# A state-space scan with a two-layer block: prefix products in one scan, W_out parts by adding transfers, a new order on every engine

## The chip, the core and the metric

The kernel runs on one core of a Trainium2 chip. The core has TensorE (PE; its weight loads are listed apart as PEld), VectorE (DVE), ScalarE (ACT), GpSimd (POOL) and SyncE (SP), which here only issues transfers. Each engine takes its instructions in the order of its own queue and waits at semaphores for the others. The metric is the device time of one execution in microseconds (us); the median of three runs of the kernel before is 332.77 us (331.59 to 333.74).

## What is computed

```python
# x (4, 8, 768, 32), a (4, 8, 768), B and C (4, 8, 768, 16)
log_a = np.log(np.clip(a, 1e-06, 1.0))
for c in range(nc):                                   # chunks of 32 steps
    cum = np.cumsum(la, axis=-1)
    L = np.exp(cum[:, :, :, None] - cum[:, :, None, :]) * causal
    CB = np.einsum('bhin,bhjn->bhij', Cc, Bc)
    y_intra = np.einsum('bhij,bhjd->bhid', CB * L, xc)
    y_inter = np.einsum('bhin,bhnd->bhid', Cc, state) * np.exp(cum)[:, :, :, None]
    y[:, :, sl] = y_intra + y_inter
    Bx = np.einsum('bhjn,bhjd->bhjnd', Bc, xc) * np.exp(cum[:, :, -1:] - cum)[:, :, :, None, None]
    state = np.exp(np.sum(la, axis=-1))[:, :, None, None] * state + np.sum(Bx, axis=2)
# then, on (4 * 768, 8 * 32) = (3072, 256)
h = x @ w_in                                          # (256, 2048)
g = h * (1.0 / (1.0 + np.exp(-h)))
out = g @ w_out                                       # (2048, 256)
```

## The kernel before

The sequence of 4 x 768 steps is cut into 12 *units* of 256 steps (four chunks of 64), three units to a batch row. The state goes from unit to unit within a row. Two units make a *pair* of 512 columns for the two layers; pair 0 is units 0 and 1.

**The order.** The whole program is written out as one list of tokens, SCHEDULE. A token such as "E,3,0" calls one small function, which issues a few instructions on one engine; each engine's queue is the list's order, cut down to its own instructions. A second table, SLOTS, says which buffer of a pool each tile takes ("s2k": 49 of 2 KB a partition, "r4k": 12, "raw": 7, "hp": 3 in PSUM).

**A unit.** "La" loads the decays (from the scratch tensor "az" in DRAM), "Ln", "Lt" and "Lx" load B, C and x, on SP's queue for the most part. "E" makes the decay masks by a scan on DVE (line 511), "T" transposes B or C on DVE (524), "B" (519) and "C" (550) scale B and C by decays on POOL, "ce" copies C for even and odd heads on ACT (545, with the constant "par"). On PE, "g0" makes the scores (584), "D" and "gd" the state's additions (570), "Y" the outputs (634 and 643). On DVE, "M" multiplies masks and scores (599) and "S" steps the state (614). For units 0 and 1 the decays are not loaded from "az" but made on the chip from a small load of "a": "A", "AT", "AU", "as", "ab" (445, 450, 454, 494 and 496, 501).

**Prefix products.** "P" (481 to 487) makes a unit's prefix products of the decays, with a 1 ahead of every chunk, by one scan on DVE over 128 partitions and 260 columns: "Lp" loads the clipped decays into "pz" (one buffer) from the scratch tensor "ac", and the scan writes "pfx" (one buffer). "ac" is filled by four "AD" stores on POOL's queue from "acp", which "AA" clips on POOL. There are ten such scans, for units 2 to 11. Units 0 and 1 have their own ("P01").

**Weights.** w_in and w_out come as 64-bit floats, in eight pieces of 512 KB each ("lw,0" to "lw,15", the first eight of them w_in). A piece goes through "u" and "v" on ACT (294, 297), "w,n,0", "w,n,1" and "w,n,2" on DVE (303, 307, 310) and "W" on POOL (318) to become 32-bit floats. For products at full pace each piece is then split in three parts: high "H" on ACT (322), low "lD" and third "dD" on DVE (326, 330).

**Layers.** Pair 0's first layer runs in plain 32 bits: "s" (696), 12 groups of 8 products, and its second layer "n1" (760), 64 products, all but two pieces of w_in, which go as for the later pairs. From there each pair has eight steps "a" (8 products, 799, high and low parts), "ax" on ACT (810), "d" (4 products, third part), "dg" (silu, 820) and "h" (826) on ACT, "l" (650) and "e" (836) on DVE, and then "q" (781): three products for each of 2 x 8 x 2 groups, in the accumulators "hp" and "o_ps". "Va" and "Vd" add the accumulators up, "o" (714) transposes, "O" stores. The last half pair is turned over on PE ("Vt", "ot", "or", "os", lines 726 to 749).

**Fillers.** "z" issues products of a tile of zeros into "o_ps": its first number is how many wide ones (128 x 512, line 438), the second how many narrow ones (64 x 64, line 440).

**Names on the path of the prediction.** The first weight step, the first scan of unit 0, its second mask product ("M,0,0"), the first group of first-layer products ("s,0,0"), unit 1's scan ("E,1,0"), and the fourth group of first-layer products, with which an unbroken run of first-layer products begins.

Of the kernel before, what the change touches and what calls it, by code (L numbers as in the profile page):

```python
# [35 lines left out]
T,3,0 Ln,3,0,1,0 Lx,3,1,0 Lp,3,0 P,3 n1,2,1 Ln,3,0,0,0 B,3 gd,3 w,12,2 W,12 Lt,4,0,0,0 lD,6 y,2,1 xh,2 g0,3 M,3,0 b,3,1
C,3 b,3,0 n1,10,1 n1,3,0 a,0,6 w,10,1 W,10 Lt,4,0,3,0 lD,0 S,3,0 S,3,1 M,3,1 dD,6 n1,11,0 H,13 S,3,2 Lp,4,0 w,14,0
Lt,4,1,0,0 w,14,1 Lx,4,1,0 ax,0,6 n1,10,0 x,2,1 H,15 SM,3,0 d,0,6 w,14,2 H,8 n1,5,0 La,4,1,0 n1,9,0 x,2,0 lD,5 La,4,0,0
E,4,0 Ln,4,0,1,0 dg,0,6 SM,3,1 Y,3 y,3,1 y,3,0 xh,3 lD,3 W,14 H,14 n1,13,0 n1,12,0 T,4,1 ce,4,0 n1,5,1 lD,9 n1,9,1 x,3,0
a,1,0 ax,1,0 n1,13,1 dD,5 Lt,4,0,2,0 x,3,1 n1,8,1 Lt,4,0,1,0 T,4,0 lD,1 ce,4,1 S,3,3 dD,0 d,1,0 P,4 C,4 n1,11,1 E,4,1  # L40
dg,1,0 lD,8 n1,12,1 dD,8 H,10 Lt,5,0,1,0 g0,4 Lx,4,0,0 Ln,4,0,0,0 B,4 H,4 gd,4 b,4,0 dD,1 M,4,1 b,4,1 S,4,0 S,4,1 S,4,2
SM,4,1 n1,4,0 M,4,0 Lt,5,1,1,0 SM,4,0 lD,4 Lt,5,1,0,0 lD,2 S,4,3 dD,2 h,1,0 dD,3 l,1,0 e,1,0 n1,8,0 n1,4,1 Vn,0 lD,10
Y,4 y,4,0 n1,0,1 y,4,1 a,1,1 xh,4 dD,10 H,12 lD,12 Vn,1 Lt,5,0,0,0 ax,1,1 a,1,2 ax,1,2 Lt,5,1,2,0 d,1,1 dg,1,1
Ln,5,0,0,0 Lt,5,1,3,0 T,5,1 La,5,1,0 o,0,0,2 q,1,0,0,1 La,6,1,0 ce,5,1 La,5,0,0 Ln,5,0,1,0 d,1,2 dg,1,2 h,1,2 ce,5,0
Lt,6,1,2,0 a,1,3 ax,1,3 q,1,0,1,1 a,1,4 ax,1,4 d,1,3 dg,1,3 Lp,5,0 q,1,0,1,0 E,5,1 E,5,0 B,5 o,0,1,2 lD,13 AD,2 lD,11
dD,4 Lx,5,0,0 l,1,2 e,1,2 d,1,4 dg,1,4 q,1,2,1,0 q,1,0,0,0 Lt,5,0,2,0 Lt,5,0,3,0 T,5,0 lD,15 dD,12 g0,5 x,4,1 Lx,5,1,0
Ln,6,0,0,0 gd,5 P,5 M,5,1 h,1,4 h,1,1 l,1,4 q,1,2,0,1 a,1,5 q,1,2,1,1 e,1,4 q,1,4,0,1 q,1,2,0,0 La,6,0,0 b,5,0 S,5,0
AD,3 Lt,6,1,1,0 q,1,4,0,0 b,5,1 ax,1,5 d,1,5 Ln,6,0,1,0 S,5,1 S,5,2 SM,5,0 M,5,0 SM,5,1 dD,13 Lt,6,1,3,0 x,4,0 q,1,4,1,1
q,1,4,1,0 C,5 dD,9 dg,1,5 h,1,5 Y,5 Lp,6,0 y,5,1 l,1,1 y,5,0 e,1,1 q,1,1,1,1 a,1,7 O,0,0,2,1,0 l,1,5 Lt,6,1,0,0
q,1,1,0,1 q,1,1,0,0 ax,1,7 e,1,5 d,1,7 Lt,6,0,0,0 xh,5 q,1,5,1,0 E,6,1 Lx,6,0,0 q,1,5,0,1 dg,1,7 Lt,6,0,3,0 T,6,1 ce,6,1  # L50
P,6 x,5,0 ce,6,0 Lt,6,0,2,0 Lt,6,0,1,0 T,6,0 q,1,5,0,0 E,6,0 h,1,7 C,6 g0,6 B,6 M,6,1 Lx,6,1,0 gd,6 b,6,0 Lt,7,1,2,0
h,1,3 q,1,1,1,0 S,6,0 M,6,0 dD,15 b,6,1 q,1,5,1,1 a,2,1 ax,2,1 S,6,1 S,6,2 SM,6,1 a,1,6 ax,1,6 l,1,7 e,1,7 q,1,7,0,0
q,1,7,0,1 d,1,6 dD,11 x,5,1 Lt,7,0,1,0 q,1,7,1,1 q,1,7,1,0 dg,1,6 d,2,1 l,1,3 e,1,3 lD,14 q,1,3,0,0 h,1,6 Lt,7,1,3,0
q,1,3,0,1 SM,6,0 l,1,6 dg,2,1 h,2,1 Y,6 La,7,1,0 y,6,0 e,1,6 Lt,7,1,0,0 Lx,7,1,0 S,6,3 Lt,7,1,1,0 T,7,1 ce,7,0 y,6,1
xh,6 Lt,8,1,0,0 q,1,3,1,1 dD,14 a,2,0 ax,2,0 q,1,6,1,0 q,1,6,1,1 ce,7,1 q,1,6,0,0 l,2,1 d,2,0 Ln,7,0,0,0 dg,2,0 h,2,0
Lp,7,0 P,7 O,0,1,2,0,0 e,2,1 q,1,6,0,1 x,6,1 Va,1,1 x,6,0 q,1,3,1,0 Lt,7,0,2,0 Vd,1,1 o,1,1,2 Lx,7,0,0 a,2,3 ax,2,3
Va,1,0 Vd,1,0 a,2,2 Lt,7,0,3,0 q,2,1,0,1 q,2,1,0,0 l,2,0 o,1,0,2 e,2,0 ax,2,2 d,2,2 q,2,1,1,0 d,2,3 q,2,0,0,0 dg,2,3
q,2,0,1,1 dg,2,2 h,2,2 q,2,1,1,1 La,7,0,0 E,7,0 Lt,7,0,0,0 O,0,1,2,2,0 O,0,0,2,3,0 q,2,0,0,1 C,7 T,7,0 g0,7 Ln,7,0,1,0
E,7,1 B,7 h,2,3 gd,7 b,7,0 M,7,1 O,0,1,2,3,0 q,2,0,1,0 a,2,5 b,7,1 ax,2,5 S,7,0 S,7,1 M,7,0 l,2,2 e,2,2 La,8,0,0 a,2,4
# [67 lines left out]
def kernel(  # L127
# [231 lines left out]
    def pz01(u):  # L359
        return held(f"pz{u}", [128, 4, Q + 1])  # L360
# [527 lines left out]
```

## Time and profile before

| | |
|---|---|
| median of three runs | 332.77 us (331.59 to 333.74) |
| the profiled execution's own time | 333.58 us |
| its span, from the first instruction to the last | 331.8 us |
| TensorE clock granted, mean over the span | 0.985 |
| PE instructions, DVE, ACT, POOL | 3078, 350, 309, 64 |
| read from DRAM, written to it | 22.81 MB, 3.34 MB |
| DVE, longest waits in total | 28.9 us for ACT at line 650, 8.0 us for PE at line 599 |
| last transfers to the output, from issue to landing | 1.8 us |

The profile shows one execution. A group's row gives its busy time and the mean length of one instruction, then the idle time of its engine just ahead of it and what ended that. Products are pipelined: one of 512 columns is listed with some 390 ns, and the next may start long before it ends. So the pace of products is read from the length of a run of them in the chain that ended last, and not from the mean.

### The profile page before, as it was taken

Reading aid. Unit: us, or ns where it says so; the run is one execution under the profiler, and the core shown is the slowest. Engines: PE = TensorE matmul, PEld = TensorE weight load, DVE = VectorE, ACT = ScalarE, POOL = GpSimd, SP = SyncE. Lnnn points to the kernel's source line nnn. Section 1 sums busy time; section 2 is a strip of 40 time slices with the busy share of each in tenths; the row PEclk is TensorE's granted clock in tenths of the full one; section 3 lists DMA queues with packets and bytes.
Section 4 is the critical chain, followed back from the end, with each engine's and each line's share of the span. In section 5 each row is a group of like instructions: output and inputs, shape, how many; then the busy total and the mean of one; then the engine's idle time right before and its main releaser. Section 6 shows DMA issues by size and latency. Waiting matters only on the chain.

```text
span 331.8 us, 7522 instructions
## 1 busy us (share of the span) xinstructions
PE 321.9 (97%) x3078; PEld 244.0 (74%) x3078; DVE 250.8 (76%) x350; ACT 204.9 (62%) x309; POOL 48.6 (15%) x64
## 2 busy tenths in 40 slices
PE   6799999999999999999999999999999999999995
PEld 2478874455587878787887887877888787878884
DVE  4887899999999989698966678956486845453663
ACT  4669787644777565766566677726576367674811
POOL 2435565341111010010010100010000000000000
PEclk9769999999999999999999999999999999999999
DMA  5999478342253311245227241250003300031002
GB/s 173 218 276 256 173 202 197 63 94 34 69 117 69 73 48 21 53 109 123 29 38 152 73 89 30 38 111 2 2 9 70 58 2 0 2 54 18 2 0 63
DMA packets 93522, 26.64 MB, mean 80 GB/s; under 512 B 79840, under 2 KB 86752, under 8 KB 93488
## 3 DMA queue, kind: packets, MB, share of 16 engines
q1 hardware_dynamic: 90960, 25.71, 34.3%
q10 hardware_dynamic: 2352, 0.26, 0.6%
q8 instruction: 24, 0.39, 0.5%
q0 software_dynamic: 176, 0.20, 0.3%
q14 instruction: 10, 0.08, 0.1%
HBM read 22.81 MB, written 3.34 MB: 79 GB/s over the span
## 4 chain that ended last, share of the span: by engine, by line
PE 78%; DVE 12%; DMA 4%; ACT 2%; issue 1%; SPq 1%; POOL 1%; DVEq 0%; POOLq 0%
PE hp L781 27%; PE ga L799 15%; PE gb L799 15%; PE o_ps L781 5%; PE hp L696 5%; PE hp L760 3%; DVE ab L511 3%; PE ga L634 2%; PE ga L584 2%; PE ga L643 1%; DVE ab L599 1%; DMA bn<-in_B_dram 1%; DVE s2k L330 1%; DVE s2k L326 1%; DMA tbc<-in_C_dram 1%
## 5 line engine op out<-in xcount | busy, mean ns | idle before, releaser
L781 PE MATMUL hp<-r4k,s2k 128*128 128x512 f32 x400 | 109.5, 394 | 0.0
L781 PEld LDWEIGHTS hp<-r4k,s2k 128*128 128x128 f32 x400 | 74.0, 188 | 16.4 <-issue 0.5
L650 DVE SCALAR_TENSOR_TENSOR r4k<-r4k,r4k 128x1024 fp32r<-128x1024 f32 (+1 forms) x42 | 50.4, 1199 | 36.6 <-ACT r4k L826 28.9
L799 PE MATMUL ga<-raw,s2k 128*128 128x512 f32 x240 | 62.1, 394 | 0.0
L799 PE MATMUL gb<-raw,s2k 128*128 128x512 f32 x240 | 62.0, 393 | 0.1
L799 PEld LDWEIGHTS gb<-raw,s2k 128*128 128x128 f32 x240 | 44.5, 188 | 11.6 <-ACT gb L810 1.2
L799 PEld LDWEIGHTS ga<-raw,s2k 128*128 128x128 f32 x240 | 44.6, 188 | 11.3 <-ACT ga L810 1.2
L836 DVE SCALAR_TENSOR_TENSOR r4k<-r4k,r4k 128x1024 fp32r<-128x1024 f32 x40 | 48.7, 1222 | 4.9 <-PE o_ps L781 1.5
L826 ACT ACTIVATE r4k<-r4k 128x1024 fp32r<-128x1024 f32 x40 | 41.9, 1057 | 2.0 <-PE hp L781 0.5
L810 ACT ACTIVATE ga<-ga 128x1024 f32<-128x1024 f32 x21 | 21.2, 1009 | 20.5 <-PE ga L799 20.5
L820 ACT ACTIVATE r4k<-gb 128x1024 f32<-128x1024 f32 x21 | 21.5, 1025 | 15.6 <-PE gb L799 15.4
L810 ACT ACTIVATE gb<-gb 128x1024 f32<-128x1024 f32 x21 | 21.2, 1008 | 15.6 <-PE gb L799 15.6
L820 ACT ACTIVATE r4k<-ga 128x1024 f32<-128x1024 f32 x21 | 21.5, 1024 | 15.0 <-PE ga L799 13.8
L781 PE MATMUL o_ps<-r4k,s2k 128*128 128x512 f32 x80 | 30.7, 390 | 0.0
L760 PE MATMUL hp<-r4k,s2k 128*128 128x512 f32 x64 | 30.1, 602 | 0.0
L318 POOL TENSOR_TENSOR s2k<-s2k,s2k 128x512 uint32<-128x512 uint32 (+1 forms) x19 | 24.1, 1280 | 22.6 <-DVE s2k L310 13.7
L519 POOL TENSOR_TENSOR BT<-bn,ab 128x256 f32<-128x256 f32 x10 | 7.3, 730 | 120.3 <-DVE ab L511 87.5
L511 DVE TENSOR_TENSOR_SCAN ab<-ab,diag 128x512 f32<-128x512 f32 x20 | 24.8, 1246 | 0.0
L696 PE MATMUL hp<-r4k,s2k 128*128 128x256 f32 x96 | 22.9, 395 | 0.0
L696 PEld LDWEIGHTS hp<-r4k,s2k 128*128 128x128 f32 x96 | 18.7, 199 | 3.4 <-issue 0.4
L760 PEld LDWEIGHTS hp<-r4k,s2k 128*128 128x128 f32 x64 | 11.6, 189 | 10.8 <-issue 9.3
L599 DVE TENSOR_TENSOR ab<-gb,ab 128x512 f32<-128x512 f32 x12 | 8.2, 686 | 12.3 <-PE gb L584 7.4
(123 smaller groups left out, 390.9 us busy)
## 6 DMA issues: line engine op xcount, KB each, us to landing
ab<-az SPq DMA_DIRECT2D x20, 256.0 KB, 4.2
raw<-in_moe_w_in_dram SPq DMA_DIRECT2D x8, 512.0 KB, 4.1
raw<-in_moe_w_out_dram SPq DMA_DIRECT2D x8, 512.0 KB
out_dram<-r4k SPq DMA_DIRECT2D x44, 64.0 KB, 2.9
xt<-in_x_dram SPq DMA_DIRECT2D x20, 128.0 KB, 2.6
pz<-ac SPq DMA_DIRECT2D x10, 130.0 KB
bn<-in_B_dram SPq DMA_DIRECT2D x20, 64.0 KB, 3.6
tbc<-in_C_dram SPq DMA_DIRECT2D x36, 32.0 KB, 3.7
```

The source lines that it names most:

```text
L318: nc.gpsimd.tensor_tensor(out=u[:, :, fs], in0=u[:, :, fs], in1=v[:, :, fs], op=ALU.add)
L511: nc.vector.tensor_tensor_scan(out=o, data0=src, data1=diag.rearrange("p h t -> p (h t)"), initial=0.0, op0=ALU.mult, op1=ALU.add)
L599: nc.vector.tensor_tensor(out=o, in0=DP[u][w][:, :, 0:256].rearrange("p g (k x) -> p k g x", k=2), in1=o, op=ALU.mult)
L650: nc.vector.scalar_tensor_tensor(out=l, in0=f32(h), scalar=BACK, in1=y, op0=ALU.mult, op1=ALU.add)
L696: nc.tensor.matmul(out=hp[:, i], lhsT=WT[j][:, kc, 128 * i:128 * i + 128], rhs=XM()[:, 2 * kc:2 * kc + 2, u], start=(kc == 0), stop=(kc == ...
L760: nc.tensor.matmul(out=NP[m], lhsT=WT[8 + f // 2][:, f % 2, 128 * m:128 * m + 128], rhs=GT[0, f // 2][:, f % 2], start=(n == 1), stop=(n = ...
L781: nc.tensor.matmul(out=ACC[P, c], lhsT=WK[8 + i, p][:, k, 128 * m:128 * m + 128], rhs={"h": HT, "l": LT, "d": DT}[p][P, i][:, k], start=(n ...
L799: nc.tensor.matmul(out=o, lhsT=WK[j, q][:, kc, 128 * i:128 * i + 128], rhs=xs[:, 2 * kc:2 * kc + 2], start=(start and q == "h" and kc == 0 ...
L810: nc.scalar.activation(t, t, AF.Copy, scale=1.0 + Z)
L820: nc.scalar.activation(g, t, AF.Silu, scale=BACK)
L826: nc.scalar.activation(t, GT[G, i], AF.Copy, scale=-LESS * Z)
L836: nc.vector.scalar_tensor_tensor(out=DT[G, i], in0=f32(HT[G, i]), scalar=-1.0, in1=f32(LT[G, i]), op0=ALU.mult, op1=ALU.subtract)
```

## The change

The diff has three parts beside the two tables, which are new throughout.

- **One scan.** "P", "pz" and the constant "one" of 260 columns go. A token "AP" scans "acp" once (48 partitions, 8 heads of 65 columns) before the stores to "ac"; "Lp" loads finished prefix products into "pfx", which has two buffers now.
- **Adding transfers.** Low parts of pieces 10 to 15 and third parts of pieces 12 to 15 are no longer made by "lD" and "dD" on DVE. "Wl" and "Wd" copy the high part on ACT with a scale, and "Wm" and "We" add the other term by a transfer that POOL's queue issues with an adding target. The functions were there before and not called; the third part's transfer reads the low part as its source.
- **Zeros.** 11 wide and 36 narrow fillers become 36 wide ones: ten ahead of "AT", two behind it, 23 more up to "s,0,0", and one behind "Y,1".

In the new order the loads of unit 0's B stand first on ACT's queue; "a" stands ahead of the first weight on SP's queue; the pieces of weights come as 0, 4, 7, 5, 1, 12, 13, 8, 15, 14, 6, 10, 2, 3, 9, 11 (before: 4, 0, 5, 3, 2, 1, 11, 7, 9, 8, 15, 13, 6, 10, 12, 14); "par" is made among DVE's first instructions.

```diff
--- before.py
+++ after.py
 SCHEDULE = """
-cp cI c1 lw,4 ci z,1 z,1 z,1 z,1 ia,0 ct v,4 ia,1 z,1 z,1 z,0,6 z,1 cd ip,0,0 z,1 co u,4 ca A AT AU as,1,0 lw,0 ir,0 z,1
-as,0,0 ab,0,0 ch P01,0,0 P01,0,1 w,4,0 E,0,0 Lt,0,1,2,0 z,1 Lt,0,1,1,0 Ln,0,0,1,1 Ln,0,0,0,1 B,0,0 z,0,6 z,0,6 as,0,1
-ab,0,1 z,0,6 v,0 w,0,2 Lt,0,1,0,0 Lt,0,1,3,0 T,0,1 C,0 Ln,1,0,0,0 ir,3 Lx,0,0,0 tp,0 as,1,1 Lx,0,1,0 ab,1,0 E,0,1 u,0
-w,0,0 w,0,1 tq,0 B,0,1 cP ce,0,1 lw,5 ce,0,0 E,1,0 Ln,1,1,0,0 z,1 W,0,1 D,0 S,0,0 v,5 W,0,0 B,1,0 S,0,1 S,0,2 SM,0,1
-z,0,6 g0,0 M,0,1 Lt,3,1,0,0 M,0,0 lw,3 u,5 SM,0,0 v,3 w,5,0 w,5,1 u,3 w,5,2 S,0,3 ab,1,1 E,1,1 Ln,1,1,1,0 Y,0 X0,0,1
...
+Ln,0,0,0,1 ia,1 ci z,1 z,1 z,1 z,1 z,1 z,1 ia,0 Ln,0,0,1,1 cI z,1 ch cP ct ip,0,0 z,1 z,1 z,1 c1 cd A AT cp AU lw,0 z,1
+z,1 as,0,0 ab,0,0 P01,0,0 P01,0,1 as,0,1 ab,0,1 as,1,1 ab,1,1 E,0,0 u,0 z,1 z,1 z,1 Lt,0,1,3,0 v,0 w,0,0 w,0,2 w,0,1
+lw,4 W,0,1 z,1 B,0,0 z,1 z,1 v,4 Lt,0,1,1,0 u,4 z,1 z,1 Ln,1,1,1,0 z,1 E,0,1 B,0,1 z,1 z,1 z,1 Lt,0,1,0,0 Lt,0,1,2,0
+T,0,1 as,1,0 z,1 z,1 z,1 tp,0 tq,0 E,1,1 Lx,0,0,0 Lx,0,1,0 D,0 S,0,0 z,1 w,4,2 z,1 S,0,1 z,1 w,4,0 S,0,2 ce,0,0 ce,0,1
+g0,0 M,0,1 lw,7 v,7 Ln,1,0,0,0 SM,0,0 M,0,0 z,1 z,1 SM,0,1 u,7 w,4,1 w,7,0 z,1 z,1 w,7,2 w,7,1 lw,5 v,5 w,5,2 W,0,0
+S,0,3 Ln,1,1,0,0 ab,1,0 E,1,0 C,0 Y,0 X0,0,1 Ln,1,0,1,0 B,1,1 X0,0,0 u,5 w,5,0 ip,1,0 z,1 P01,1,0 tp,1 tq,1 s,0,0 ce,1,1
+ce,1,0 g0,1 Lx,1,1,0 Lx,1,0,0 W,4 xh,0 w,5,1 si,0,0 B,1,0 P01,1,1 D,1 s,0,4 M,1,1 lw,1 u,1 lw,12 S,1,0 W,5 v,1 ca S,1,1
+S,1,2 SM,1,0 SM,1,1 lw,13 s,0,5 si,0,5 v,12 C,1 M,1,0 Y,1 w,1,0 w,1,1 W,7 si,0,4 lw,8 w,1,2 W,1,0 z,1 w,12,2 X0,1,0 H,7
...
-    one = const.tile([128, 4, Q + 1], FP32, name="one")
...
     def load_pz(u, q):
         q = QUEUES[q]
-        PZ[u] = keep("pz", [128, 4, Q + 1], loads)
+        PFX[u] = keep("pfx", [128, 4, Q + 1], loads2, u % 2)
         b, t0 = at(u)
         c0 = t0 // Q * (Q + 1)
-        q.dma_start(out=PZ[u].rearrange("p c t -> p (c t)"),
+        q.dma_start(out=PFX[u].rearrange("p c t -> p (c t)"),
...
+    def one():
+        return held("one", [NCH, H, Q + 1], key="r4k")
...
     def c_one():
-        nc.gpsimd.memset(one, 0.0)
-        nc.gpsimd.memset(one[:, :, 0:1], 1.0)
+        nc.gpsimd.memset(one(), 0.0)
+        nc.gpsimd.memset(one()[:, :, 0:1], 1.0)
...
-    def f_P(u):
-        PFX[u] = keep("pfx", [128, 4, Q + 1], loads)
-        nc.vector.tensor_tensor_scan(out=PFX[u].rearrange("p c t -> p (c t)"),
-                                     data0=PZ[u].rearrange("p c t -> p (c t)"),
-                                     data1=one.rearrange("p c t -> p (c t)"), initial=0.0,
+    def f_AP():
+        t = acp().rearrange("p h t -> p (h t)")
+        nc.vector.tensor_tensor_scan(out=t, data0=t, data1=one().rearrange("p h t -> p (h t)"), initial=0.0,
                                      op0=ALU.mult, op1=ALU.add)
```

Functions of the kernel before that are called now:

```python
    def w_part(n, p):                                  # tokens Wl, Wd
        t = WK[n, p] = small(f"{p}{n}", [128, 2, WF], FR)
        nc.scalar.activation(t, f32(WK[n, "h"]), AF.Copy, scale=1.0 if p == "l" else Z)

    def w_more(n, p):                                  # tokens Wm, We
        other = WT[n] if p == "l" else f32(WK[n, "l"])
        nc.gpsimd.dma_start(out=f32(WK[n, p]).rearrange("p k f -> p (k f)"),
                            in_=other.rearrange("p k f -> p (k f)"), accum_op=ALU.add)
```

More of the change, by code (lines that the diff above doesn't have):

```diff
@@ L212, in f32 @@
         return t.bitcast(FP32)
-    bn, tbc, xt, E, M, BT, BH, CT, CE, CW, PFX, ST, SM, DP, BX, YS, PZ = ({} for _ in range(17))
+    bn, tbc, xt, E, M, BT, BH, CT, CE, CW, PFX, ST, SM, DP, BX, YS = ({} for _ in range(16))
     def at(u):
@@ L842 @@
         "AA": f_AA, "AD": f_AD, "z": busy, "as": f_AS, "ab": f_Ab, "E": lambda u, *k: f_E(u, k or (0, 1)),
-        "P01": f_P01, "P": f_P, "T": f_T, "tp": f_TP, "tq": f_TQ, "ce": f_T2, "B": f_B, "C": f_C,
+        "P01": f_P01, "AP": f_AP, "T": f_T, "tp": f_TP, "tq": f_TQ, "ce": f_T2, "B": f_B, "C": f_C,
         "D": lambda u: f_D0(u, True), "g0": f_G0, "gd": f_D0, "b": f_BX, "M": f_M, "S": f_S, "SM": f_SM,
```

160 lines of the change are left out of this document (79 added, 81 removed), and 6 rows, old and new, of the table SLOTS.

## The prediction

> **What bounds the kernel now.** I read the page first, then the windows, then the windows of single source lines, then the timelines of the first 30 us.
>
> ```profile
> span 331.8 us, 7522 instructions
> PE 321.9 (97%) x3078; PEld 244.0 (74%) x3078; DVE 250.8 (76%) x350; ACT 204.9 (62%) x309; POOL 48.6 (15%) x64
> ...
> DVE  4887899999999989698966678956486845453663
> ...
> PEclk9769999999999999999999999999999999999999
> ```
>
> Two engines look full: PE to the end, DVE from about 40 to 110 us (slices of 8.3 us). The granted clock dips in the second and third slice only. A busy PE is not a PE at its peak, so I counted its work. The windows cut the run where the second run of first-layer products (L696) begins, 29.04, and where the last product of the second layer ends, 327.02; below them the same middle window, asked of one source line each: L696, L760, L781, L799, then the four lines of small products, L584, L570, L634, L643 (first figure length, second PE busy, then PEld):
>
> ```profile
> 20.00:29.04 9.04, 9.04 (x185) 7.12 (x184) 7.74 (x19) 6.81 (x15) 3.27 (x3) 0.88 1.06 336
> 29.04:327.02 297.98, 297.22 (x2674) 227.49 (x2668) 227.37 (x293) 187.18 (x274) 38.60 (x41) 1.00 0.30 65
> 327.02:331.80 4.78, 1.23 (x10) 0.82 (x10) 1.31 (x5) 0.38 (x1) 0.00 (x0) 1.00 0.50 110
> ...
> 29.04:327.02 297.98, 16.14 (x72) 13.52 (x72) 1.00 0.30 65
> 29.04:327.02 297.98, 30.06 (x64) 11.56 (x64) 1.00 0.30 65
> 29.04:327.02 297.98, 121.71 (x480) 89.01 (x480) 1.00 0.30 65
> 29.04:327.02 297.98, 127.04 (x504) 93.42 (x504) 1.00 0.30 65
> ...
> 29.04:327.02 297.98, 6.93 (x320) 4.52 (x320) 1.00 0.30 65
> 29.04:327.02 297.98, 4.44 (x288) 2.83 (x288) 1.00 0.30 65
> 29.04:327.02 297.98, 6.59 (x296) 5.21 (x296) 1.00 0.30 65
> 29.04:327.02 297.98, 8.65 (x646) 6.96 (x640) 1.00 0.30 65
> ```
>
> Their pace, back to back, from the chain that ended last (start, length, what):
>
> ```profile
> 29.11 8.84 PE hp L696 x40
> ...
> 71.36 1.72 PE hp L760 x4
> ...
> 163.20 1.81 PE hp L781 x8
> ```
>
> So 0.221, 0.430 and 0.226 us each (L799 is the same 512-wide form as L781). In the middle window: 72 x 0.221 + 64 x 0.430 + 984 x 0.226 = 15.9 + 27.5 + 222.4 = 265.8 us, and the small products 26.6: 292.4 of 297.98. At most 5.6 us of 298 are not work. All of it must still be done after the change, so from 29 us on the change can win 5.6 us and no more, however much it takes off DVE. What is left is the first 29 us, where PE does 24 of the 96 L696 products and two small units, and the last 4.8.
>
> **The change part by part.** Rows for what is swapped (groups, then DMA issues with KB and us to landing):
>
> ```profile
> L326 DVE TENSOR_TENSOR s2k<-s2k,s2k 128x512 fp32r<-128x512 f32 x16 | 13.2, 836 | 0.6 <-ACT s2k L322 0.6
> L330 DVE SCALAR_TENSOR_TENSOR s2k<-s2k,s2k 128x512 fp32r<-128x512 f32 x16 | 12.2, 771 | 0.1
> L322 ACT ACTIVATE s2k<-s2k 128x512 fp32r<-128x512 f32 x16 | 9.8, 626 | 0.0
> L483 DVE TENSOR_TENSOR_SCAN pfx<-pz,one 128x260 f32<-128x260 f32 x10 | 7.2, 716 | 2.5 <-DMA pz<-ac 2.5
> ...
> 42.32 1.60 POOL L467 DMA_DIRECT2D ac<-r4k  x2
> ...
> ab<-az SPq DMA_DIRECT2D x20, 256.0 KB, 4.2
> ```
>
> *Scans.* Ten scans of 260 columns (7.2 us) become one of 520 columns on 48 partitions: twice the columns, some 1.4 us. DVE saves 5.8. It now stands ahead of the stores to "ac", and DVE waits in it for POOL (clip and a larger memset); behind it are weight steps of DVE, which run well ahead of PE there. The loads keep their number and bring finished products.
>
> *W_out parts.* Six low parts and four third parts leave DVE: 6 x 0.836 + 4 x 0.771 = 8.1 us. ACT gets ten copies, 6.3 us, POOL ten issues of about 0.8 us (1.60 for two), and the queues ten adding transfers of 256 KB. ACT goes from 62% to 64%, POOL from 15% to 17% of the span. DVE saves 13.9 us in all; behind the 5.6 us of the middle nearly all of that is cover. I take 0.3 us of gain there (bounds 0 and 5.6; the near one, because L326 and L330 were hidden behind products already).
>
> *Zeros.* 11 wide and 36 narrow products of zeros become 36 wide. They matter through the clock and where they stand in PE's order: 35 come before the first real product of L696, one between the first three groups of it and the rest, none later.
>
> *Start.* The rows of before: products of zeros cold and warm, the load of "a", DVE's order up to the second mask product (L599), and what POOL and ACT waited for:
>
> ```profile
> 1.94 2.74 PE L438 MATMUL o_ps<-s2k 128*128 128x512 bf16 x6 [1.94 <-DVE s2k L385]
> 5.07 0.62 PE L438 MATMUL o_ps<-s2k 128*128 128x512 bf16 x2
> 4.54 0.21 DVE L445 TENSOR_SCALAR s2k<-s2k 32x128 f32<-32x128 f32 x1 [1.61 <-DMA s2k<-in_a_dram]
> 7.41 0.40 DVE L303 TENSOR_SCALAR s2k<-s2k 128x512 f32<-128x512 f32 x1
> 7.72 1.22 DVE L511 TENSOR_TENSOR_SCAN ab<-hp,diag 128x512 f32<-128x512 f32 x1
> 9.69 0.69 DVE L310 SCALAR_TENSOR_TENSOR s2k<-raw,s2k 128x512 uint32<-128x512 uint32 x1 [0.75 <-ACT s2k L297]
> 10.30 0.64 DVE L524 STREAM_TRANSPOSE ct<-s2k 128x256 f32<-128x256 f32 x1
> 10.78 1.16 DVE L511 TENSOR_TENSOR_SCAN ab<-hp,diag 128x512 f32<-128x512 f32 x1
> 14.72 0.60 DVE L614 SCALAR_TENSOR_TENSOR st<-st,s2k,hp 128x64 f32<-128x64 f32 x2
> 16.30 0.68 DVE L599 TENSOR_TENSOR ab<-ga,ab 128x512 f32<-128x512 f32 x1
> 16.90 0.42 DVE L303 TENSOR_SCALAR s2k<-s2k 128x512 f32<-128x512 f32 x1
> 17.35 0.43 DVE L307 TENSOR_SCALAR s2k<-s2k 128x512 uint32<-128x512 uint32 x1
> ...
> 11.35 0.41 POOL L519 TENSOR_TENSOR BT<-s2k,ab 128x128 f32<-128x128 f32 x1 [7.76 <-DMA s2k<-in_B_dram]
> 13.31 1.41 POOL L318 TENSOR_TENSOR s2k<-s2k,s2k 128x256 uint32<-128x256 uint32 x2 [0.37 <-DVE s2k L307]
> 13.40 0.91 ACT L545 ACTIVATE ce<-ct,par 128x256 f32<-128x256 f32 x2 [1.29 <-DVE par L419]
> ...
> 20.20 2.82 PE hp L696 x8
> ```
>
> The new order puts unit 0's B loads at the head of ACT's queue (POOL's 7.76 us wait for B goes; what is late next is DVE's scan), "par" among DVE's first instructions (ACT's 1.29 us wait goes), and "a" ahead of the first weight on SP. "a" gains little: ten cold products of zeros at up to 0.46 us (2.74 for 6), from 1.2 on, stand ahead of its transpose and end by 5.8, where the last ones ahead of it ended at 5.69 before. The weight step at 7.41 no longer stands ahead of the first scan, which I put at 7.3. From there DVE's queue sets the start. Steps, start to start in these rows: scan 1.15, L303 0.45, L310 0.6, L307 0.45, transpose 0.5, state step 0.3, mask product 0.6. After the first scan come, in the new order, L303, L310, L307, scan, transpose, scan, state, L310, state, L303, state, two mask products: 1.15 + 0.45 + 0.6 + 0.45 + 1.15 + 0.5 + 1.15 + 0.3 + 0.6 + 0.3 + 0.45 + 0.3 + 1.2 = 8.6, so the second mask product ends at 15.9; before, 16.30 + 0.68 = 16.98. I add 0.3 for steps that run beside POOL and stretch: 16.2.
>
> From there to the first L696 group it took 20.20 - 16.98 = 3.2 us before, at a clock of half speed. If the clock holds, I estimate 1.9 (the same work at double pace, but for ACT's two copies): 18.1, a gain of 2.1. The first group took 2.82 before; at 0.221 it takes 1.77. Behind it, though, unit 1's state product waits for DVE's fourth scan, which the new order puts after five weight steps: 16.2 + 5 x 0.5 + 0.3 + 1.15 = 20.2, and POOL's 0.41 behind it: 20.7, against a PE that is free at 18.1 + 1.77 + 0.7 (scores of unit 1, L584: 6.93 for ten units) = 20.6. The extra 1.05 us is kept nearly whole. Two more groups (3.5), 0.4 of state products and unit 1's output products (1.5) bring PE to 26.1. That group also needs a weight from DVE: from 20.2 five weight steps (2.4), a clip and a prefix scan (0.95), three state steps (0.9) and three products of masks and prefixes (1.55) take it to 26.0, and POOL's half addition, 0.7, to 26.7. So the group that began at 29.04 begins at 26.8: 2.2 us gained, bounds 0.5 (everything stretches) and 3.
>
> *End.* The last products, the transposes and the stores are the same kinds in another order; the 4.8 us behind 327.02 stay. Six narrow zeros there go and nobody waited for them.
>
> Sum: -2.2 (start) - 0.3 (middle) + 0 (end) = -2.5: span 329.3. The profiled execution took 333.58 us, 1.78 more than its span and 0.8 above the median of 332.77, so 331.1 on its scale and **330.3** on the median's.
>
> *The clock, by row and by rule.* The clock was full in the first slice, after six zeros in a row, and 0.7 and 0.6 in the next two, where the zeros were narrow and far apart. The Trainium skill, "TensorE: Matmul & The Clock Gate", Part 1, says that an idle PE is throttled by default, that about 3.4 us of sustained work release it, and that one idle window of that length throttles it again; the trace agrees with the dip, and with 0.46 against 0.31 us per zero. By that rule the 25 zeros from 6 to 15 us hold the clock.
>
> *The adding transfers, by row and by rule.* Two issues on POOL took 1.60 us at 42 us, in a slice where DVE reads 9. The Trainium skill, "SBUF — State Buffer", Summary, says that descriptor generation for transfers issued from GpSimd starves under some DVE modes; no row here shows it, and by it the issues alone would last longer, with the price of the third rival.
>
> **The rivals.**
> 1. *The clock is not held* (zeros too thin, or the gate's window falls badly). Then the 1.05 of the first group is lost, the 1.3 between mask product and group too, and seven zeros between unit 0's state and output products cost 7 x 0.2 more: -2.5 + 3.75 = +1.2, **334.0**. For it: the dip that before has. Against: 35 wide zeros up to there, where before had 11 wide and 30 narrow ones.
> 2. *DVE was the bound after all.* Its slices read 8 and 9 from 40 to 110 us; if all of the middle's 5.6 us were waits on DVE, they go: 330.3 - 5.3 = **325.0**. Against: the chain's back-to-back pieces there.
> 3. *Slower: the adding transfers land late.* PE takes its products in order; part 14 needs two in a row (its third part adds its low part). They can start once POOL has done unit 6's B, and are needed after six second-layer groups (6 x 3 x 0.226), three first-layer groups (3 x 8 x 0.226), two third parts (2 x 0.90) and one unit's output (1.5): 12.8 us. Two issues and landings, 2 x (0.8 + L), pass that from L = 5.6. One plain passage of 256 KB lands in 4.2; an addition reads source and target and writes, two to three passages, 8.4 to 12.6. At L = 10.5 PE stands 9.8 us: **340.1**; the result is over 1% slower from L = 8.5. Behind the waiting issue on POOL stand unit 7's B and C products. Against: passages overlap, and DMA engines are 30% busy.
> 4. *The start does not shorten* (loads contend at a DMA share of 1.06 from 20 to 29 us, or DVE's steps stretch like POOL's neighbours): **332.5**.
>
> **How the numbers follow.** Forecast 0.46 (own range 328.5 to 332), rival 1 0.17, rival 2 0.14, rival 3 0.13, rival 4 0.10. A measurement of this kernel tells about 1%, 3.3 us, from no change: faster is below 329.4, slower above 336.1. Faster: half of the forecast's share, 0.23, and rival 2: 0.37. Slower: rival 3, 0.13. Within: the rest, 0.50. The range leaves out rival 3 and the far half of rival 2: 326.5 to 334.5.
>
> **What would show it.** Right: (lines of the new kernel stand one lower) PEclk at 9 from the second slice on; no long wait of POOL for B; the first product of the first layer near 18.1 and the fourth group near 26.8; after that PE's pieces back to back, end minus fourth group unchanged near 298. DVE busy near 237, ACT near 211. Wrong: a gap in PE ahead of second-layer products that a transfer ends (rival 3); PEclk below 9 in slices 2 and 3 (rival 1); the stretch from the fourth group to the end shorter by more than 2 us (rival 2).

## The result and the profile after

| | before | after |
|---|---|---|
| median of 13 runs each | 332.82 us (331.22 to 334.19) | 330.25 us (328.70 to 333.83) |
| the profiled execution's own time | 333.58 us | 329.10 us |
| its span | 331.84 us | 327.38 us |
| first group of first-layer products | 19.99 | 17.94 |
| fourth group | 29.04 | 26.41 |
| fourth group to the end of the second layer | 297.96 us | 295.80 us |
| from there to the end of the span | 4.8 us | 5.2 us |

The ratio of the times is 0.9916, with a 95% interval of 0.9894 to 0.9938: 2.8 us less. That is inside the 1% that the prediction counted as no change, though the interval lies wholly below 1. The predicted 330.3 is met to 0.1 us. The spans of the two profiled executions, however, lie 4.46 us apart, where the medians lie 2.57 apart, and the section on the reasons has to say why.

The page of the kernel after, its engines, two of its slice rows, the chain by engine, and the row of the adding transfers (issues, KB each, us from issue to landing):

```profile
span 327.4 us, 7519 instructions
PE 320.3 (98%) x3064; PEld 243.4 (74%) x3067; DVE 240.4 (73%) x331; ACT 209.5 (64%) x319; POOL 56.0 (17%) x74
...
DVE  4998999999988965877687299665787544635553
...
PEclk9999999999999999999999999999999999999999
...
PE 94%; SPq 2%; DMA 1%; DVE 1%; issue 1%; DVEq 0%
...
s2k<-s2k POOLq DMA_DIRECT2D x10, 256.0 KB, 3.8
```

DVE has lost 10.4 us of busy time, not the 13.9 that I forecast (the swapped steps themselves give 15.5, the others take 5.1 longer), and is as full as before up to 110 us; the clock's dip in the second and third slice is gone; the chain is PE for 94% of the span. The adding transfers land in 3.8 us in the median, under the 5.6 us from which my third rival would have decided; the slowest of the ten took 5.9.

The timelines of the start answer to those shown of before: the first zeros (PE), "a" clipped, the first scan, the second scan, the second mask product and unit 1's scan (DVE), POOL's first two operations, the copies with "par" (ACT), and the first and fourth run of first-layer products:

```profile
1.27 4.45 PE L441 MATMUL o_ps<-s2k 128*128 128x512 bf16 x10 [1.27 <-DVE s2k L388]
...
4.10 0.22 DVE L448 TENSOR_SCALAR s2k<-s2k 32x128 f32<-32x128 f32 x1 [0.41 <-DMA s2k<-in_a_dram]
7.50 1.20 DVE L512 TENSOR_TENSOR_SCAN ab<-hp,diag 128x512 f32<-128x512 f32 x1
9.87 1.22 DVE L512 TENSOR_TENSOR_SCAN ab<-hp,diag 128x512 f32<-128x512 f32 x1
14.90 0.69 DVE L600 TENSOR_TENSOR ab<-ga,ab 128x512 f32<-128x512 f32 x1
18.21 1.22 DVE L512 TENSOR_TENSOR_SCAN ab<-hp,diag 128x512 f32<-128x512 f32 x1
...
10.04 0.73 POOL L318 TENSOR_TENSOR s2k<-s2k,s2k 128x256 uint32<-128x256 uint32 x1 [6.81 <-DVE s2k L307]
10.73 0.85 POOL L520 TENSOR_TENSOR BT<-s2k,ab 128x128 f32<-128x128 f32 x2
...
12.21 0.91 ACT L546 ACTIVATE ce<-ct,par 128x256 f32<-128x256 f32 x2
...
17.94 1.99 PE L697 MATMUL hp<-r4k,s2k 128*128 128x256 f32 x8
26.41 1.89 PE L697 MATMUL hp<-r4k,s2k 128*128 128x256 f32 x8 [0.16 <-issue]
```

POOL no longer stands for B (its first work now waits for DVE's weight step, and its first B product begins at 10.73, not 11.35), ACT no longer for "par"; the second mask product ends at 14.90 + 0.69 = 15.59 where before it ended at 16.98. The first group of products took 3.03 us in this view before and takes 1.99 now, with the clock held.

The windows of after, cut at the same two places (length, then PE, PEld, DVE, ACT and POOL busy, clock, DMA share, GB/s):

```profile
17.94:26.41 8.47, 8.19 (x187) 6.55 (x186) 7.30 (x17) 6.01 (x13) 6.22 (x8) 1.00 0.86 255
26.41:322.21 295.80, 295.80 (x2668) 228.12 (x2667) 218.56 (x276) 193.40 (x287) 45.21 (x52) 1.00 0.40 79
322.21:327.35 5.14, 0.73 (x4) 0.48 (x4) 1.31 (x5) 0.38 (x1) 0.00 (x0) 0.94 0.53 102
```

In the middle PE is busy for the whole 295.80 us, against 297.22 of 297.98 before, and the list of PE's waits there is empty. Over the 292.4 us of work that the prediction counted, 3.4 us are now left, where 5.6 were. Of the 2.2 us that the middle won, only 0.76 were idle time of PE before; the other 1.4 lie inside runs of products that the windows count as busy, and no row shows what held them there.

### The profile page after: what moved, and what is told of

It reads as the page before. It is cut to its first block, busy times and chain, and to the rows that moved or that the text cites. A ratio compares the mean times of both kernels' runs of the same rounds, so it can differ in the third digit from the quotient of the medians.

```text
span 327.4 us, 7519 instructions
## 1 busy us (share of the span) xinstructions
PE 320.3 (98%) x3064; PEld 243.4 (74%) x3067; DVE 240.4 (73%) x331; ACT 209.5 (64%) x319; POOL 56.0 (17%) x74
## 4 chain that ended last, share of the span: by engine, by line
PE 94%; SPq 2%; DMA 1%; DVE 1%; issue 1%; DVEq 0%
PE hp L782 29%; PE ga L800 18%; PE gb L800 18%; PE hp L761 9%; PE hp L697 6%; PE o_ps L782 6%; PE ga L635 2%; PE ga L585 2%; PE ga L644 2%; DMA s2k<-in_C_dram 1%; PE gb L644 1%; PE ga L571 1%; SPq L262 0%; SPq L375 0%; PE o_ps L531 0%
## 5 line engine op out<-in xcount | busy, mean ns | idle before, releaser
L800 PE MATMUL gb<-raw,s2k 128*128 128x512 f32 x240 | 61.1, 390 | 0.0
L761 PEld LDWEIGHTS hp<-r4k,s2k 128*128 128x128 f32 x64 | 11.6, 189 | 10.5 <-issue 9.6
L782 PEld LDWEIGHTS o_ps<-r4k,s2k 128*128 128x128 f32 x80 | 15.0, 188 | 3.2
```

Of the source, the lines that this page charges most:

```text
L761: nc.tensor.matmul(out=NP[m], lhsT=WT[8 + f // 2][:, f % 2, 128 * m:128 * m + 128], rhs=GT[0, f // 2][:, f % 2], start=(n == 1), stop=(n = ...
L782: nc.tensor.matmul(out=ACC[P, c], lhsT=WK[8 + i, p][:, k, 128 * m:128 * m + 128], rhs={"h": HT, "l": LT, "d": DT}[p][P, i][:, k], start=(n ...
L800: nc.tensor.matmul(out=o, lhsT=WK[j, q][:, kc, 128 * i:128 * i + 128], rhs=xs[:, 2 * kc:2 * kc + 2], start=(start and q == "h" and kc == 0 ...
```

## The experiments

Each kernel ran beside the kernel before on the same chip. The table gives the fourth group and the middle of each one's profiled execution, the median, and the ratio to the kernel before.

| run | fourth group | middle | median | ratio, 95% interval |
|---|---|---|---|---|
| before | 29.04 | 297.96 | 332.82 | |
| after | 26.41 | 295.80 | 330.25 | 0.9916 (0.9894 to 0.9938) |
| e1_narrow_zeros | 27.27 | 295.82 | 330.94 | 0.9940 (0.9916 to 0.9964) |
| e2_parts_on_dve | 26.56 | 298.35 | 332.14 | 0.9982 (0.9958 to 1.0006) |
| e3_scans_per_unit | 26.32 | 306.91 | 339.21 | 1.0201 (1.0146 to 1.0255) |
| e4_zeros_behind_a | 27.07 | 295.82 | 331.38 | 0.9947 (0.9918 to 0.9977) |
| e5_scans_in_place | 26.04 | 298.88 | 332.47 | 0.9985 (0.9959 to 1.0010) |
| e6_order_alone | 26.87 | 302.34 | 336.79 | 1.0124 (1.0091 to 1.0156) |
| e7_b_load_late | 35.44 | 295.61 | 337.93 | 1.0153 (1.0121 to 1.0184) |
| e8_parts_alone | 27.84 | 309.61 | 345.68 | 1.0388 (1.0355 to 1.0421) |
| e9_b_early_before | 26.92 | 297.99 | 331.66 | 0.9970 (0.9948 to 0.9992) |
| e10_wide_before | 27.31 | 298.50 | 333.02 | 1.0017 (0.9991 to 1.0043) |
| e11_both_before | 27.62 | 298.55 | 331.98 | 0.9977 (0.9954 to 0.9999) |
| e12_a_first | 28.94 | 298.47 | 333.59 | 1.0045 (1.0018 to 1.0072) |

### The middle: the parts, the scans, the order

*The parts back on DVE.* The changed kernel, with the ten parts made by DVE where the transfers stood:

```diff
-        t = WK[n, p] = small(f"{p}{n}", [128, 2, WF], FR)
-        nc.scalar.activation(t, f32(WK[n, "h"]), AF.Copy, scale=1.0 if p == "l" else Z)
+        WK[n, p] = small(f"{p}{n}", [128, 2, WF], FR)
...
-        nc.gpsimd.dma_start(out=f32(WK[n, p]).rearrange("p k f -> p (k f)"),
-                            in_=other.rearrange("p k f -> p (k f)"), accum_op=ALU.add)
+        if p == "l":
+            nc.vector.tensor_tensor(out=WK[n, "l"], in0=f32(WK[n, "h"]), in1=WT[n], op=ALU.add)
+        else:
+            nc.vector.scalar_tensor_tensor(out=WK[n, "d"], in0=f32(WK[n, "h"]), scalar=Z, in1=f32(WK[n, "l"]),
+                                           op0=ALU.mult, op1=ALU.add)
```

> The changed kernel with the ten W_out parts made on DVE again, at the places where the transfers were issued; the ten copies on ACT go. If DVE's work was cover behind TensorE: within 0.8 us of the changed kernel, the stretch from the fourth group of first-layer products to the last product within 0.8 us of what it is there. If the 2 us that this stretch lost came from DVE's 8.1 us: it grows back by 1 to 4 us and the time with it.

The middle grew by 2.55 us, the whole gain of the middle and a little more. PE's waits in it (engine and line that waited, for what, us in total, times, longest):

```profile
PE ga L636 <- ACT sm L624: 1.0, 1, 1.0
PE hp L783 <- DVE r4k L838: 0.4, 1, 0.4
PE ga L801 <- DVE s2k L326: 0.3, 1, 0.3
```

Behind ACT's "sm" stands a state step of DVE, for which ACT waits 1.8 us there. So 8.1 us of DVE's time, spread over parts that are hidden one by one, push DVE's other steps past the moment at which PE asks for them. These rows are 1.7 of the 2.55 us; the rest is not put down to a step.

*The scans back, one buffer.* The changed kernel with ten scans, one "pz" and one "pfx" as before, and each load of "pz" right behind the scan that frees it:

```diff
-        PFX[u] = keep("pfx", [128, 4, Q + 1], loads2, u % 2)
+        PZ[u] = keep("pz", [128, 4, Q + 1], loads)
...
+    def f_P(u):
+        PFX[u] = keep("pfx", [128, 4, Q + 1], loads)
```

> The changed kernel with ten scans of 260 columns on DVE, one for each unit just ahead of its first use, and single buffers for loads and products as before; the one scan goes. If DVE's work was cover: within 0.8 us of the changed kernel, though a scan that waits for its load may cost up to 2.5 us where unit 2 begins. If the scans held the middle: 1 to 4 us slower, with the middle stretch longer by as much.

The middle grew by 11.1 us, far more than the scans' own time. SP's issues around the second load of "pz" (line 240), and the scan that frees its buffer:

```profile
47.17 0.45 SPq L272 DMA_DIRECT2D xt<-in_x_dram  x1
57.13 0.62 SPq L240 DMA_DIRECT2D pz<-ac  x1
58.34 0.62 SPq L232 DMA_DIRECT2D ab<-az  x1
...
56.41 0.69 DVE L490 TENSOR_TENSOR_SCAN pfx<-pz,one 128x260 f32<-128x260 f32 x1
```

and in the timeline what DVE then waited for:

```profile
64.71 2.34 DVE L518 TENSOR_TENSOR_SCAN ab<-ab,diag 128x512 f32<-128x512 f32 x2 [4.14 <-DMA ab<-az]
```

SP issued nothing from 47.6 to 57.13, when the scan had ended (56.41 + 0.69 = 57.10), and the loads of the next unit's decays, B and C stood behind it on the same queue; PE stopped twice, for 2.4 and 2.7 us, and the clock halved from 69.3 to 76.1. This run told two things at once, the scan's time and the buffer, so the next one parts them.

*The scans back, in place.* Each scan now works in place in one of the two load buffers, just ahead of its first use; every load keeps its place:

```diff
     def f_P(u):
         nc.vector.tensor_tensor_scan(out=PFX[u].rearrange("p c t -> p (c t)"),
                                      data0=PFX[u].rearrange("p c t -> p (c t)"),
```

> The changed kernel with ten scans of 260 columns again, but each done in place in one of the two load buffers, so that every load keeps its place and its buffer, and the SyncE queue has nothing to stand at. DVE gets back 10 x 0.68 - 1.23 = 5.6 us (durations of the run with scans per unit). Theory A (what DVE saves is worth about 0.31 of it in the middle, as 8.1 us were worth 2.55 with the parts back on DVE): the stretch from the fourth group to the end of the second layer 295.8 + 1.8 = 297.6, median near 332.0. Theory B (the middle's DVE time is cover, as I predicted): 295.8 to 296.1, median 330.3 to 330.6. Theory C (the 11 us of the scans per unit with one buffer came from the scan's own wait for its load, not from the queue): 300 or more. Fourth group near 26.4 in all of them, clock held.

The middle grew by 3.1 us: theory A in kind, and above it in size (1.8); C is out, the 8 us between this run and the last come with the single buffer. Two rows of PE's waits are 2.0 of the 3.1 us:

```profile
PE ga L576 <- POOL BT L525: 1.6, 1, 1.6
PE ga L805 <- DVE ab L605: 0.4, 1, 0.4
```

The 1.6 us are a queue's work: POOL's product of C waits 4.93 us for DVE's scan (5.08 in the run that follows, whose rows are shown there), and its product of B, which PE needs, stands behind it on POOL. 3.1 us is the price at this place; no run tried a scan placed earlier.

*The order alone.* Both edits together (parts on DVE, scans in place), so that the new order does the old work.

> The changed kernel's order with neither of its two savings: ten scans in place, and the ten parts on DVE without copies and transfers. DVE's busy time is then that of the kernel before, near 251 us. Theory A (DVE time counts): the middle stretch 295.8 + 2.55 + 1.8 = 300.1, median near 334.5, slower than before though the start is 2.6 us shorter. Theory B (cover, the order does it): 296 to 298, median 330.5 to 332. Fourth group near 26.5 in both.

PE's waits in the middle:

```profile
PE ga L577 <- POOL BT L526: 1.6, 1, 1.6
PE hp L788 <- DVE r4k L843: 1.5, 2, 1.3
PE ga L641 <- ACT sm L629: 1.2, 1, 1.2
PE ga L806 <- DVE ab L606: 0.4, 1, 0.4
```

POOL's timeline ahead of the first of them:

```profile
66.78 0.68 POOL L557 TENSOR_TENSOR cw<-ct,pfx 128x256 f32<-128x256 f32 x1 [5.08 <-DVE pfx L490]
67.41 0.64 POOL L526 TENSOR_TENSOR BT<-bn,ab 128x256 f32<-128x256 f32 x1
```

and the window of the middle:

```profile
26.87:329.21 302.34, 297.34 (x2669) 227.64 (x2667) 231.33 (x295) 187.79 (x277) 37.60 (x42) 1.00 0.31 67
```

The middle is 302.34, 6.5 us above the changed kernel and 4.4 above the kernel before, and the kernel is slower than before by 1.24%. DVE's work in the middle is 231.3 us here and 227.4 before: with a start that ends earlier, more of DVE's work falls behind it. So the new order is no gain in the middle; it is one that needs the savings, and with them PE stops waiting altogether.

*The parts alone.* The other half of that question: the kernel before with "lD" of pieces 10 to 15 and "dD" of 12 to 15 replaced in their places by copy and adding transfer.

> The kernel before with one part of the change alone: the low parts 10 to 15 and the third parts 12 to 15 by a copy on ACT and an adding transfer, at the places where DVE made them. DVE saves 8.1 us, ACT gets 6.3. Theory A (0.31 of what DVE saves): the middle stretch 297.96 - 2.5 = 295.5, median near 330.3. Theory B (cover): 297.7, median 332.5. Theory C (the order of before does not leave a transfer its 0.8 + 3.8 us from issue to landing, and POOL or PE stands for it): 298.5 or more, median 333.4 or more, with waits of PE or DVE that a transfer from s2k to s2k ends. Fourth group near 29.0.

Theory C, at a price that I had not put down: the middle 309.61, the median up by 3.9%. The transfers' line gives the time from issue to landing:

```profile
DMA to landing us min/median/max: 3.2/4.6/6.0
```

PE's waits for them:

```profile
PE hp L783 <- DMA s2k<-s2k: 4.5, 1, 4.5
PE o_ps L783 <- DMA s2k<-s2k: 2.6, 1, 2.6
```

The timelines show PE's two stops, and POOL's issue ahead of the second:

```profile
111.15 0.77 PE L783 MATMUL o_ps<-r4k,s2k 128*128 128x512 f32 x1 [2.62 <-DMA s2k<-s2k]
146.93 1.62 PE L783 MATMUL hp<-r4k,s2k 128*128 128x512 f32 x3 [4.47 <-DMA s2k<-s2k]
...
142.39 0.85 POOL L341 DMA_DIRECT2D s2k<-s2k  x1 [5.47 <-ACT s2k L337]
```

and a window lays the clock (the third figure from the end) beside it:

```profile
144.90:151.80 6.90, 4.87 (x12) 3.85 (x13) 3.05 (x4) 0.00 (x0) 1.48 (x1) 0.51 0.86 158
```

The last transfer is issued at 142.39, after POOL has waited 5.47 us for ACT's copy, and PE stands from 142.5 to 146.9 for it. Each stop also costs the clock: it is half for 3.4 us from 110.8 and for 6.8 us from 144.9. In the changed kernel the same ten transfers land in 3.8 us and PE waits for none of them; POOL does, twice, for 5.8 us in all, ahead of issuing the next one.

### The start: zeros, the loads of B and a

*Narrow zeros.* The changed kernel with the 26 zeros behind "AT" made narrow again ("z,1" to "z,0,1").

> The changed kernel with the 26 wide zeros behind the transpose of a made narrow (64 x 64). If the wide zeros hold the clock: the granted clock falls to a half somewhere between 9 and 23 us, the first group of first-layer products takes some 2.8 us in place of 1.85, the fourth group begins at 27.5 to 30 in place of 26.4, and the time is 1.5 to 3.7 us above the changed kernel's. If the zeros only fill gaps and the new order alone made the start shorter: no dip that matters, the fourth group within 0.4 us of 26.4, the time within 0.7 us.

```profile
12.50:19.30 6.80, 6.19 (x152) 4.88 (x138) 6.14 (x15) 4.17 (x10) 2.03 (x3) 0.50 0.87 190
```

In this window of the run the clock, third from the end, is half, and the fourth group comes 0.86 us later; the middle stays at 295.82. All twelve timed executions show a mean clock of 0.990 or less, so the width of the zeros does hold the clock in this order. The price, some 0.7 us of the median, is not clear of the noise: the intervals of this run and of the changed kernel overlap.

*Fewer zeros ahead of "AT".* Three of the ten moved behind "AU".

> The changed kernel with three of the ten zeros ahead of the transpose of a put behind it. The data of a are clipped at 4.43 us, but the transpose starts only behind the tenth zero, near 5.4. If these zeros hold the start: the transpose and all of DVE's chain come 0.7 to 1.1 us earlier, and so do the fourth group and the end; the time falls by 0.7 to 1.1. If the clock's release or the first weight's landing (used at 7.27) holds it: less than 0.3 us.

The transpose of "a" came earlier (4.83 instead of 5.65), but the clock was released only at 8.8 instead of 5.9, the products behind ran at half pace, and the fourth group came 0.66 us later. The seven profiles of this order with all ten zeros ahead have the release between 4.5 and 5.9. So the zeros ahead of the transpose are not merely in its way; they bring the release forward. But this is one profile; the five in which the start is unchanged (after, e2, e3, e5, e6) have the fourth group anywhere from 26.04 to 26.87, and the intervals of the two ratios overlap: a loss in time is not shown, only that there is no gain of 0.7 to 1.1.

*B's loads late.* The changed kernel with unit 0's two loads of B back ahead of its B products in ACT's queue:

```diff
-Ln,0,0,0,1 ia,1 ci z,1 z,1 z,1 z,1 z,1 z,1 ia,0 Ln,0,0,1,1 cI z,1 ch cP ct ip,0,0 z,1 z,1 z,1 c1 cd A AT cp AU lw,0 z,1
+ia,1 ci z,1 z,1 z,1 z,1 z,1 z,1 ia,0 cI z,1 ch cP ct ip,0,0 z,1 z,1 z,1 c1 cd A AT cp AU lw,0 z,1
...
-lw,4 W,0,1 z,1 B,0,0
+lw,4 W,0,1 z,1 Ln,0,0,1,1 Ln,0,0,0,1 B,0,0
```

> The changed kernel with unit 0's two B loads back ahead of the first B products in ACT's queue, as the kernel before had them. By the step of my prediction (the early load is one of the three things that shorten the start) POOL's first B product begins later than 10.73 and the fourth first-layer group moves from 26.41 to 26.7 or later. By the rival (the load was never what the start waited for, DVE's queue was) the group stays within 0.2 us of 26.41. Middle stretch near 295.8 in both.

ACT's issue and POOL's first B product in its timelines:

```profile
10.73 1.16 ACTq L256 DMA_DIRECT2D s2k<-in_B_dram  x2
...
18.75 0.78 POOL L522 TENSOR_TENSOR BT<-s2k,ab 128x128 f32<-128x128 f32 x2 [8.05 <-DMA s2k<-in_B_dram]
```

The fourth group came at 35.44: 9.0 us later. The loads were issued at 10.73, though ACT's last operation ahead of them ended at 8.46 (the profile shows nothing that held them), and landed 8.0 us after that; before, issued at 7.34, they landed in 4.0. POOL, PE and DVE stood for them one after another. In this order the early load is no small term but a condition.

*The pieces of the start in the kernel before.* Three runs put them there one by one: B's loads (and "hm", "par" and the memset of the zeros) early; its five groups of six narrow zeros ahead of "s,0,0" made four wide ones each; both; and both with "a" ahead of the first weight on SP.

> The kernel before with one part of the new start: unit 0's two B loads at the head of ACT's queue, the memset of the zeros first on DVE, and the two small constants (hm, par) made early; its zeros stay narrow. If the early load is a gain by itself: POOL's first B product near 8.9 instead of 11.35 (right behind the first scan), the fourth group at 28.2 to 28.7 instead of 29.04, clock still at half speed from about 12 to 22 us. If the load is worth something only where the queues are as full as in the new order: 28.8 to 29.1. Middle 298 in both.

> The kernel before with its narrow zeros ahead of the first first-layer products (five groups of six) made into five groups of four wide ones, nothing else. If the zeros' width is what holds the clock: no half-speed stretch from 12 to 22 us, fourth group at 27.5 to 28.3 instead of 29.04. If POOL's late B leaves PE idle too long for any zeros there: the half-speed stretch stays in part, fourth group at 28.5 or later. Middle 298.

> Both edits of the two runs before in the kernel before: early B load and wide zeros. If the new start is these two and no more: fourth group near 26.4 to 27.0 as in the changed kernel, a gain of 2 to 2.6. If the order of DVE's steps (second scan ahead of the weight steps) is the larger part: 27.3 to 28.0. Middle 298, median 330.5 to 332.

> The run before (early B load and wide zeros in the kernel before) with the load of a ahead of the first weight on SyncE's queue, as the new order has it. If the early B load pushed the load of a back (DVE's clip of a at 4.57 with wide zeros alone, 6.71 with both) and this is what took the second gain away: the clip at 4.0 to 4.8 again, DVE's first scan near 7.5 to 8.2 instead of 9.21, fourth group at 26.2 to 26.9. If it is the cold zeros ahead of the transpose of a: first scan at 8.8 or later, fourth group at 27.3 or later. Middle 298.

The first two brought the fourth group of their profiled executions forward by 2.1 and 1.7 us, both together by 1.4, all three by 0.1. They do not add up. (The profile of before, from which these gains are counted, lost three stretches at half clock, as the section on the reasons shows. In the ratios only the early load, 0.9970, and both, 0.9977, gain, and the third is slower, 1.0045.) With both, "a" was clipped at 6.71, where with wide zeros alone it was clipped at 4.57; B's loads now go ahead of it. With "a" in front of the weight it was clipped at 4.09, as I had put it, but the row behind shows what paid:

```profile
7.51 0.29 DVE L474 TENSOR_SCALAR s2k<-s2k 128x256 f32<-128x256 f32 x1 [1.22 <-DMA s2k<-in_a_dram]
...
14.98 0.68 ACT L299 ACTIVATE s2k<-raw 128x512 f32<-128x512 uint32 x1 [2.45 <-DMA raw<-in_moe_w_in_dram]
16.80 0.27 PE L636 MATMUL ga<-cw,sm 32*64 32x64 f32 x2 [1.03 <-ACT sm L624]
```

The second load of "a" and the weights came later, ACT stood 2.45 us for a weight with its copies for PE behind it. Neither theory of that run was right: the numbers fall on the second one's side (28.94), but the transpose behind the cold zeros came early, at 5.35. A load moved ahead moves another back here; in the kernel before the share of the transfer engines that is busy is 0.82 over the first 20 us. The changed kernel's start is one order that fits together, and its gain can't be given to one of its pieces.

## Why the prediction was right, and where it was not

**The bound, right.** PE from the fourth group on was the bound, and the middle could win 5.6 us at most. It won 2.2; by the prediction's own sign (a stretch near 298 us that gets shorter by more than 2) that speaks for the second rival.

**The start, right in the two profiles.** Forecast 16.2 for the second mask product, 18.1 for the first group, 26.8 for the fourth; the profile after has 15.59, 18.09 (in the chain, from which 18.1 was worked out; 17.94 in the timeline) and 26.41. The first scan was put at 7.3 and came at 7.50, unit 1's fourth scan began at 18.21 where I had 19.05. The early B load, "par" and the held clock are each seen in their row. That "a" gains little agrees with 4.10 against 4.54.

**The middle, wrong in size.** The step that failed is "I take 0.3 us of gain there ... because L326 and L330 were hidden behind products already". A part is hidden where it stands, but DVE is one queue: what the part delays is the step behind it, a state step in the run with the parts, a scan or a mask in others. The runs put 2.55 us of the middle on the parts and 3.1 on the scans at the places tried, 6.5 together, of which the new order had first lost 4.4. The balance, 6.54 - 4.38 = 2.16, is the middle's gain. The second rival, DVE as the bound, was thus half true.

**The end, 0.3 us.** I had put nothing; the new order's last steps take 5.17 us instead of 4.84.

**The third rival, right in kind.** Its landing of 10.5 us was an estimate of two to three passages; it measured 3.8 here, 5.9 at most, and 4.6 in the old order. What it describes happened there: PE took its products in order and stood 7.1 us for two transfers. The point from which it decides hangs on the places, and not on the landing alone.

**The other rivals.** The clock was held in the changed kernel (mean clock 0.997 or more in 11 of its 13 executions), so the first one fell. The fourth, a start that does not shorten, fell in the two profiles; in the medians it is not far off, as follows.

**The sum, right by two errors, which is luck.** The terms of the profiles are -2.63, -2.16 and +0.33: -4.46, where I had -2.5; the medians give -2.57. The profiled execution of before is not like its median. Each execution's mean clock is listed with its time. (The list of the clock begins with its first release, at 5.13 us in the profile of before, so the cold zeros ahead of it are not in the mean.) One stretch of 3.4 us at half clock takes 0.5% from a mean over 331 us, so the 84 executions of the kernel before that ran beside the experiments fall apart by the number of such stretches:

| mean clock | stretches at half clock | executions | mean time |
|---|---|---|---|
| 0.997 to 1.000 | 0 | 28 | 331.74 us |
| 0.992 to 0.995 | 1 | 20 | 332.44 us |
| 0.987 to 0.990 | 2 | 18 | 333.23 us |
| 0.981 to 0.985 | 3 | 18 | 334.15 us |

The profiled execution (0.985) lost three, the mean loses 1.3, a third of them none. The window of the profile before, and its neighbour at full clock, show the three:

```profile
5.13:11.96 6.83, 4.15 (x38) 2.62 (x38) 5.24 (x10) 3.37 (x7) 0.61 (x2) 1.00 1.02 227
11.96:22.20 10.24, 9.25 (x174) 6.59 (x172) 9.65 (x21) 6.25 (x15) 4.94 (x8) 0.50 0.95 230
```

The Trainium skill, "TensorE: Matmul & The Clock Gate", Part 1, says that the window over which activity is watched is 3413 ns long and free-running, so that one kernel finds it in another phase each time; the stretches of 3.4, 6.8 and 10.2 us in these runs and the spread over 84 executions agree.

So the clock was worth 332.74 - 331.74 = 1.0 us to the mean and not the 2.35 (1.05 and 1.3) that I read from one profile. Held against held, 331.74 and 329.89 (11 executions of the changed kernel, not run beside the 84), the change is worth 1.85. With the middle's 2.16 and the end's 0.33, that leaves nothing for the rest of the new start. This last step is worked out; no profile of the kernel before with the clock held exists that would show it. Two profiles come near, and they speak against it. In e8, whose list is that of the kernel before until far behind the start, one stretch was lost there and not three, and the fourth group came at 27.84: 0.6 us a stretch, so some 27.2 with none (an estimate); e10, with the clock held, has 27.31. The changed start has 26.04 to 26.87 in five profiles. By these the rest of the new start is worth 0.4 to 1.3 us, by the means nothing, and the runs do not settle it. The middle's term does stand on several profiles: 297.96 to 298.55 in the kernel before and the four runs that change only its start, 295.61 to 295.82 in the changed kernel and the three that change only its start. By the means, then, my two large terms had nearly changed places, -2.2 and -0.3 against about -1.0 and -2.2, and the sum came out.

What stays open, then: what the new start is worth beside the clock; which waits hide inside the busy runs of the middle; and why wide zeros in the kernel before, which held the clock in all of ten executions, gave 333.02 and not the 331.7 of its own executions with the clock held.

## What to carry to other kernels

Before a stall at the start is sized from a profile, look at the spread of the executions and their clocks: the profile may show the rarer case, and the gain is that of the mean. Time saved on an engine that looks covered is worth what is queued behind it on that engine; put the saved work back into the new order to measure it, since the order and the saving are worth little apart. A step handed from an engine to a transfer needs its whole way, issue, queue and landing, free ahead of the use: ten such transfers were worth 2.55 us of the middle in one order and cost 11.65 us of it in another.

## What the runs showed of the hardware

- In the changed kernel an adding transfer of 256 KB from one on-chip buffer to another landed in 3.8 us (3.3 to 5.9) and took POOL 0.84 to 1.18 us to issue, with DVE at 60 to 90% busy beside it; a plain one of 256 KB from DRAM ("az") landed in 4.2 us (3.7 to 4.6).
- The stretches at half clock in these profiles are one, two or three times 3.41 us long (3.4 in e8, 6.8 in e1, e3 and e8, 10.2 in the kernel before), and a stop of PE of 2.6 us inside a full program (e8, up to 111.15 us) was followed by one of them, from 110.8.
